# Local attention with 63 keys to a block, one transfer of v a head, and v pooled on TensorE for six pairs

## The chip, the cores and the metric

The kernel runs on one core of one Trainium2 chip. The metric is the device time of one execution in microseconds (us), given as the median of several runs. TensorE (PE) multiplies matrices, VectorE (DVE), ScalarE (ACT) and GpSimd (POOL) work on elements, and SyncE (SP) issues most of the DMA transfers from its own queue, in order. Each engine takes its instructions strictly in the order in which the program lists them.

## The reference

An attention layer feeds two MLP layers. Only the attention and its hand-over are touched by the change, apart from the last output tile.

```python
B, H, S, D = 4, 8, 576, 64;  factor = 4;  Sd = 144
q_d, k_d, v_d = (x.reshape(B, H, Sd, 4, D).mean(axis=3) for x in (q, k, v))
out_up = np.repeat(sm_attn(q_d, k_d, v_d), 4, axis=2)          # pooled attention, 144 x 144
mask = np.abs(pos[:, None] - pos[None, :]) < 4                  # each query sees 7 keys
out_local = softmax(where(mask, scale * q @ k.T, -1e9)) @ v     # local attention
x = (out_up + out_local) as (2304, 512)
x = silu(x @ w_in) @ w_out          # first MLP, 512 -> 2048 -> 512
return elu(x @ w_in2) @ w_out2      # second MLP
```

## The kernel before

**Attention.** The 32 heads are taken as 16 pairs (4 batches of 4 pairs), `attend(i, due)` for pair i. Rows of q and k come in, are transposed on TensorE (L653), and give two attentions. The local one cuts the 576 positions into ten windows of 64 keys, 57 apart. For each of the ten windows and two heads there is one score matmul (L773) into PSUM, a mask is added (in batch 0 by a matmul, L765), softmax runs on DVE, ACT and POOL, the result is transposed (L900) and multiplied with the window of v (L1005). Since ten windows of 64 that are 57 apart don't end at 576, the last starts at 512, and `load_windows` needs two transfers a head, one of nine windows (L614) and one of the last (L618). The pooled attention sums q and k by fours on DVE (L695), has its scores (L847), softmax, transposes (L921) and product (L939). Its v is pooled in one of two ways: for the four pairs of batch 0 (`by_pe`) by 22 matmuls (L708) from the windows already there, with a 0/1 matrix that `pool_matrix` has made as the stationary side and 64 columns of v moving; for the other twelve pairs v is loaded a second time (L608) and summed on POOL (L727, L728) or DVE (L732).

**First MLP.** Its 16 weight blocks of 512 KB (8 of w_in, 8 of w_out) are loaded into a ring of three buffers `ws` and one lent tile (L395, L400), taken apart on ACT (L426, L430) and DVE (L434, L437, L441), and split into a high and a low part (ACT L1101, POOL L1105). A unit (n, f) is 256 tokens by 256 hidden columns: the first product (L1124, 12 matmuls), silu on ACT and DVE (L1152, L1153), a split (L1155, L1158), and the second product (L1172, 12 matmuls). Units of the first tokens start when batch 0 of the attention is done and are then interleaved with the attention of the batches behind it. Six of nine token groups are done so; the rest, and the whole second MLP, follow in a second stage (L1500, L1588, L1590) that is one long run of matmuls.

**What sets the order.** Up to the second stage a list scheduler inside the program orders everything while it is built: each piece is a `Job` with an engine, a planned duration, predecessors and buffers (`Slots`) to take, and the next emitted is the one that can start first by the plan. `D_ROWS`, `D_LOCAL`, `D_V`, `D_W` are planned DMA times, `clock_of` the planned start of each engine, `STICK` a bonus for staying in one tile mode of TensorE, `MOST_H` the number of PSUM banks that first products may hold, `LENT` the weight tiles that attention and weight loads may borrow. Where the plan sees TensorE idle, `fill` puts matmuls on zeros there (L370, 128x512 bf16; nine more, `WARM`, at the start). On the chip nothing is reordered: a piece that is late holds up all that stands behind it on its engine or queue.

## Time and profile before

| | |
|---|---|
| median of 3 runs | 880.45 us (879.81 to 880.62) |
| the profiled execution | 879.63 us, its span in the profile 877.9 us |
| PE busy | 865.9 us, 99% of the span |
| DVE, ACT, POOL busy | 668.7, 543.7, 251.5 us |
| mean granted TensorE clock | 0.996 of full speed |

The time outside the span is 1.7 us. PE counts as busy while it runs fillers and while its clock is low, so 99% does not mean that it does useful work all the time. Times in the trace are counted from the start of the span.

### The profile page before, as it was taken

What the parts mean: (1) busy time and instruction counts of PE and PEld (TensorE: products, weight loads), DVE (VectorE), ACT (ScalarE), POOL (GpSimd) and SP (SyncE); (2) the same over time, 40 slices, a digit from 0 to 9 for tenths busy, and PEclk for the clock granted to TensorE, in tenths of its full rate; (3) what the DMA queues carried; (4) which work ended last, traced back from release to release, by engine and by line L of the source; (5) the groups of instructions that cost most, each with busy time, mean ns of one, the idle gap of its engine ahead of it and who ended that gap; (6) DMA issues with size and microseconds to landing.
All of it is one profiled execution on the core that took longest, in us unless ns stands there. A gap on an engine that the chain in (4) does not pass through costs nothing.

```text
span 877.9 us, 17291 instructions
## 1 busy us (share of the span) xinstructions
PE 865.9 (99%) x6632; PEld 809.7 (92%) x6640; DVE 668.7 (76%) x1255; ACT 543.7 (62%) x1228; POOL 251.5 (29%) x269
## 2 busy tenths in 40 slices
PE   8989999999999999999999999999999999999998
PEld 5779989999999999999999998898998998998986
DVE  8888777776968988979569879389489797493552
ACT  5787675564568568466377387385586684561750
POOL 4488786664103011301024213010141041010000
PEclk9989999999999999999999999999999999999999
DMA  9996377612123436253521340541420531310301
GB/s 170 205 219 173 81 202 180 169 49 97 56 90 121 132 103 221 77 173 125 178 92 52 109 156 1 166 123 60 132 72 37 174 126 37 111 70 37 108 0 72
DMA packets 105522, 100.08 MB, mean 114 GB/s; under 512 B 62240, under 2 KB 92448, under 8 KB 105312
## 3 DMA queue, kind: packets, MB, share of 16 engines
q1 hardware_dynamic: 103072, 98.39, 38.1%
q8 instruction: 52, 0.85, 0.4%
q10 hardware_dynamic: 2368, 0.59, 0.4%
q14 instruction: 30, 0.25, 0.1%
HBM read 75.37 MB, written 23.59 MB: 113 GB/s over the span
## 4 chain that ended last, share of the span: by engine, by line
PE 94%; DVE 2%; DMA 2%; issue 1%; ACT 0%; SPq 0%; POOL 0%; ACTq 0%; POOLq 0%; DVEq 0%
PE b L1500 33%; PE b L1590 22%; PE b L1588 15%; PE b L1172 8%; PE b L1124 7%; PE b L653 1%; PE b L1005 1%; PE b L921 1%; PE b L939 1%; PE b L900 1%; PE b L773 1%; PE b L847 1%; PE b L708 1%; DMA rows<-in_k_dram 1%; DMA ws<-in_moe_w_out_dram 1%; DMA rows<-in_q_dram 1%
## 5 line engine op out<-in xcount | busy, mean ns | idle before, releaser
L1590 PE MATMUL b<-w,grw 128*128 128x512 f32 x384 | 121.2, 389 | 0.0
L1590 PE MATMUL b<-w,ghk 128*128 128x512 f32 x288 | 99.1, 389 | 0.0
L1500 PE MATMUL b<-xhr,xaw 128*128 128x384 f32 x360 | 96.4, 335 | 0.0
L1588 PE MATMUL b<-grw,w 128*128 128x384 f32 x352 | 91.2, 334 | 0.0
L1590 PEld LDWEIGHTS b<-w,grw 128*128 128x128 f32 x384 | 72.1, 188 | 14.9
L1500 PE MATMUL b<-xhr,w 128*128 128x384 f32 x320 | 83.8, 335 | 0.0
L1124 PE MATMUL b<-xh,w 128*128 128x256 f32 x384 | 82.5, 293 | 1.2 <-DVE t L1153 0.7
L1172 PE MATMUL b<-gh,w 128*128 128x256 f32 x384 | 79.6, 288 | 0.0
L1590 PE MATMUL b<-w,glk 128*128 128x512 f32 x192 | 74.8, 389 | 0.0
L1588 PE MATMUL b<-ghk,w 128*128 128x384 f32 x248 | 71.6, 334 | 0.0
L1124 PEld LDWEIGHTS b<-xh,w 128*128 128x128 f32 x384 | 64.7, 194 | 3.0 <-DVE t L1153 0.9
L1500 PE MATMUL b<-xlr,xaw 128*128 128x384 f32 x200 | 66.9, 334 | 0.0
L1500 PEld LDWEIGHTS b<-xhr,xaw 128*128 128x128 f32 x360 | 65.5, 188 | 0.0
L1590 PEld LDWEIGHTS b<-w,ghk 128*128 128x128 f32 x288 | 54.1, 188 | 11.1
L1172 PEld LDWEIGHTS b<-gh,w 128*128 128x128 f32 x384 | 63.3, 191 | 0.7 <-ACT t L1152 0.2
L1588 PEld LDWEIGHTS b<-grw,w 128*128 128x128 f32 x352 | 63.7, 188 | 0.0
L1512 ACT COPY hg<-b 128x384 f32<-128x384 f32 x60 | 28.7, 480 | 52.5 <-PE b L1500 51.9
L1553 DVE SCALAR_TENSOR_TENSOR part<-b,part 128x384 f32<-128x384 f32 (+1 forms) x42 | 25.0, 609 | 44.8 <-PE b L1590 28.4
L1283 DVE TENSOR_TENSOR xlr<-tail,xhr 128x768 fp32r<-128x768 f32 x51 | 49.6, 973 | 11.5 <-ACT xhr L1280 11.2
L1500 PEld LDWEIGHTS b<-xhr,w 128*128 128x128 f32 x320 | 58.0, 188 | 0.2
L1588 PE MATMUL b<-glk,w 128*128 128x384 f32 x168 | 56.1, 334 | 0.0
L1280 ACT CAST xhr<-tail 128x768 fp32r<-128x768 f32 x60 | 50.0, 834 | 7.0 <-DVE tail L1361 4.3
(259 smaller groups left out, 2380.8 us busy)
## 6 DMA issues: line engine op xcount, KB each, us to landing
ws<-in_moe_w_in_dram SPq DMA_DIRECT2D x32, 512.0 KB
ws<-in_moe_w_out_dram SPq DMA_DIRECT2D x31, 512.0 KB
tail<-x SPq DMA_DIRECT2D x24, 384.0 KB
x<-part SPq DMA_DIRECT2D x6, 768.0 KB
out_dram<-part SPq DMA_DIRECT2D x18, 256.0 KB
vw<-in_v_dram SPq DMA_DIRECT2D x28, 144.0 KB
tail<-xd SPq DMA_DIRECT2D x10, 384.0 KB
natv<-in_v_dram SPq DMA_DIRECT2D x22, 144.0 KB
```

The source lines that it names most:

```text
L653: nc.tensor.transpose(bank.tile[:, n * TB:(n + 1) * TB], row(which, c)[:TB], ident[:TB, :TB])
L708: nc.tensor.matmul(bankv[j].tile[:HS, c * D:(c + 1) * D], pooler()[rows_, n, :], vw[rows_, w, :], start=n == 0, stop=n == len(POOLED_BY) - ...
L773: nc.tensor.matmul(held[j].tile[o:o + WIN, c:c + WIN], qT[j * D:(j + 1) * D, q0[w]:q0[w] + WIN], kT[j * D:(j + 1) * D, w0[w]:w0[w] + WIN], ...
L1124: nc.tensor.matmul(ph.tile[:, :NB0], w[a][:, c, :], x_slot(n, c, b_), start=start and m == 0, stop=stop and m == len(products) - 1,)
L1172: nc.tensor.matmul(y[d // 2].tile[:, o:o + NB0], w[m // 2][:, sl], gg(m % 2), start=f == 0 and m == 0 and d % 2 == 0, stop=fin and m == 2, ...
L1280: a = Job("A", ACT_[width], lambda: nc.scalar.copy(hi(), src), preds, gate)
L1283: other=("V", VEC_[width], lambda: nc.vector.tensor_tensor(lo(), src, hi().bitcast(F32), ALU.subtract)),
L1500: nc.tensor.matmul(acc_, a[:, cs], b[:, c, :], start=fresh and c == 0 and m == 0, stop=c == 1 and m == 2, skip_group_check=True,)
L1512: snap[after, j] = [Job("A", ACT_[NB], lambda dst=dst, acc_=acc_: nc.scalar.copy(dst, acc_), [], gate, due=soon)]
L1553: nc.vector.scalar_tensor_tensor(dst, src, sc, dst, op0=ALU.mult, op1=ALU.add)
L1588: nc.tensor.matmul(y[d][:, :NB], wm[:, sl], gm, start=first, stop=last_)
L1590: nc.tensor.matmul(y[d], gm[:, sl], wm, start=first, stop=last_)
```

## The change

Windows have 63 keys, and ten of them 57 apart end at 576, so one transfer brings all ten of a head. The score matmuls keep 64 columns except in the last window, where the 64th column lies behind the end of k: from batch 1 on two more matmuls of one column fill it with some finite score, which the mask takes out. v is pooled on TensorE for the first six pairs. The windows of v are now the stationary side, and 14 or 15 columns of a 0/1 matrix move; the result lies the other way round, so a copy, two transposes and a second copy follow (`turn_v`). Weight tiles are no longer lent to rows of q and k. First products may hold three PSUM banks. The last output tile is computed, evicted and stored in two halves, the second store from ACT's queue. Several planned durations and due times have other values.

```diff
-    PACKED, PE_POOLED, HALVED, CHUNKED, STICK, T_SECOND = 0, 1, 0, 4, 3, 40.0
+    PACKED, PE_POOLED, HALVED, CHUNKED, STICK, T_SECOND = 0, 6, 0, 4, 2, 40.0
...
-    D_ROWS, D_LOCAL, D_V, D_W, S_ROWS, S_LOCAL, X_AFTER = 1.6, 1.9, 1.5, 2.2, 1.1, 2.2, 1
+    D_ROWS, D_LOCAL, D_V, D_W, S_ROWS, S_LOCAL, X_AFTER = 1.6, 2.5, 1.9, 2.7, 1.1, 1.3, 1
...
-    SLACK, MOST_H, N_PSUM, SPLIT_F = 0.05, 2, 16, 3
-    T_MM, T_FIRST, T_PAIR = 0.1185, 38.0, 6.4
+    SLACK, MOST_H, N_PSUM, SPLIT_F = 0.05, 3, 16, 3
+    T_MM, T_FIRST, T_PAIR = 0.1185, 36.0, 6.4
...
-    w0 = [57 * i for i in range(NW - 1)] + [S - WIN]
+    KEYS = WIN - 1
+    w0 = [(KEYS - 6) * i for i in range(NW)]
...
-    LENT = {'rows': [(5, 1), (6, 0), (6, 1)], 'ws': [(7, 0)], 'v': [(7, 1)]}
+    LENT = {'ws': [(7, 0)], 'v': [(7, 1)]}
...
-    clock_of = {"A": 0.0, "V": 4.0, "G": 4.0, "S": 0.0, "P": 5.0, "dma": 0.0, "port": 4.0}
+    clock_of = {"A": 0.0, "V": 4.0, "G": 4.0, "S": 0.0, "P": 3.0, "dma": 0.0, "port": 4.0}
...
-        nc.vector.tensor_copy(m[WIN:P], m[:WIN])
...
-        by_pe = b < PE_POOLED
+        by_pe = i < PE_POOLED
...
-                    vw[j * WIN:(j + 1) * WIN, :NW - 1, :],
-                    bass.AP(tensor=rows.tensor, offset=rows.offset, ap=[[D, WIN], [w0[1] * D, NW - 1], [1, D]]),
+                    vw[j * WIN:j * WIN + KEYS],
+                    bass.AP(tensor=rows.tensor, offset=rows.offset, ap=[[D, KEYS], [w0[1] * D, NW], [1, D]]),
                 )
-                nc.sync.dma_start(vw[j * WIN:(j + 1) * WIN, NW - 1, :], rows[w0[-1]:w0[-1] + WIN, :])
...
-                for n, (w, c) in enumerate(POOLED_BY):
+                for w in range(NW):
+                    m0, m1 = pg[w], pg[w + 1]
                     for j in range(2):
-                        rows_ = slice(j * WIN, j * WIN + pool_rows(w))
                         nc.tensor.matmul(
-                            bankv[j].tile[:HS, c * D:(c + 1) * D], pooler()[rows_, n, :], vw[rows_, w, :],
-                            start=n == 0, stop=n == len(POOLED_BY) - 1, skip_group_check=True,
+                            bankv.tile[j * D:(j + 1) * D, m0:m1], vw[j * WIN:j * WIN + KEYS, w, :],
+                            pooler[j * WIN:j * WIN + KEYS, j, FAC * m0 - w0[w], :m1 - m0], start=True, stop=True, skip_group_check=True,
                         )
...
+            def turn_v():
+                for c in range(2):
+                    nc.tensor.transpose(bankt.tile[:HS, c * P:(c + 1) * P], hvt.tile[:, c * HS:(c + 1) * HS], ident)
...
+                        for c0, k0, n in [(0, w0[w], min(WIN, S - w0[w]))] + [(KEYS, S - 1, 1)] * (w == NW - 1 and b >= MASK_PE):
+                            nc.tensor.matmul(
+                                held[j].tile[o:o + WIN, c + c0:c + c0 + n],
...
+                        if final and k == FP - 1 and d == ny - 1:
+
+                            for c0, queue in ((0, nc.sync), (DM // 2, nc.scalar)):
+                                cs = slice(c0, c0 + DM // 2)
+                                for n_, (wm, gm) in enumerate(((wh, gh), (wh, gl), (wl, gh))):
+                                    nc.tensor.matmul(
+                                        y[d][:, cs], gm[:, d * P:(d + 1) * P], wm[:, cs], start=False, stop=n_ == 2, skip_group_check=True
+                                    )
...
-            prepare(i, dues[pos] - 2.5 if which == 0 else dues[pos + LAG] - 2.5)
+            prepare(i, dues[pos] - 4.0 if which == 0 else dues[pos + LAG] - 4.0)
```

The lines of the changed program have other numbers: L701 is the narrow pooling, L715 its transposes, and L773, L900, L1005, L1124, L1172 are now L776, L903, L1008, L1127, L1175; the fillers are L373.

**TensorE's order at the pooling of the first pair, before.** `rows` are q and k, `ident` makes a transpose, `t` is the zero tile of a filler (two stand here), `natv` holds the 0/1 matrix, `vw` the windows of v. L708 goes on for 22 matmuls.

```order
L921 MATMUL b_97<-ident,ring_120 72x72 x4
L653 MATMUL b_96<-ident,rows 128x96 x5
L653 MATMUL b_93<-ident,rows 128x96 x2
L370 LDWEIGHTS t
L370 MATMUL b_92<-t 128x512
L708 MATMUL b_97<-vw_116,natv 72x64
L708 MATMUL b_99<-vw_116,natv 72x64
```

The same place in the changed program. Five fillers stand where the two rows of L373 are.

```order
L645 MATMUL b_96<-ident,rows 128x96 x5
L645 MATMUL b_93<-ident,rows 128x96 x2
L373 LDWEIGHTS t
L373 MATMUL b_92<-t 128x512
L701 MATMUL b_97<-natv,vw_116 64x15 x2
L701 MATMUL b_97<-natv,vw_116 64x14 x6
L1008 MATMUL b_99<-ring_121,vw_116 64x60 x2
L1008 MATMUL b_94<-ring_121,vw_116 64x57 x2
```

Twenty matmuls with 14 or 15 columns take the place of 22 with 64, and the local product of the first pair (L1008) follows at once, where before it came after two fillers and three transposes. In all there are 60 fillers for 48, and 19 of them for 10 stand ahead of the first transposes of q.

**SP's queue from the last windows of batch 0 on, before.** `yo` and `vw` are windows of v, `ws` and `lent` weight blocks, `lent<-in_q` rows of the first pair of batch 1 in a borrowed weight tile.

```order
L614 DMA yo<-in_v_dram 64x9x64
L618 DMA yo<-in_v_dram 64x64
L400 DMA ws<-in_moe_w_out_dram 128x1024
L395 DMA ws<-in_moe_w_in_dram 128x4x256
L400 DMA lent<-in_moe_w_out_dram 128x1024
L604 DMA lent<-in_q_dram 96x6x64 x2
L604 DMA lent<-in_k_dram 96x6x64 x2
L608 DMA lent<-in_v_dram 72x512 x2
L395 DMA ws<-in_moe_w_in_dram 128x4x256
```

The same stretch in the changed program:

```order
L607 DMA yo<-in_v_dram 63x10x64 x4
L403 DMA ws<-in_moe_w_out_dram 128x1024
L398 DMA ws<-in_moe_w_in_dram 128x4x256
L403 DMA lent<-in_moe_w_out_dram 128x1024
L398 DMA ws<-in_moe_w_in_dram 128x4x256
L597 DMA nat_113<-in_q_dram 96x6x64 x2
L597 DMA nat_114<-in_k_dram 96x6x64 x2
L607 DMA vw_116<-in_v_dram 63x10x64 x2
L403 DMA ws<-in_moe_w_out_dram 128x1024
L597 DMA spare<-in_q_dram 96x6x64 x2
L398 DMA ws<-in_moe_w_in_dram 128x4x256
```

The windows of batch 0 are 8 transfers for 16. The fifth weight block (the second `L398 ws` shown) stands ahead of the rows of batch 1 instead of behind three of their transfers, and the sixth (the second `L403 ws` shown) is row 18 of the queue instead of row 41. The rows of q for pair 5 go into `spare`, which the local product of pair 3 still reads, and the seventh block stands right behind them.

## Rows read from the trace of the kernel before


**Rows 1.** Page of the profile, part 1, TensorE's line

```profile
PE 865.9 (99%) x6632; PEld 809.7 (92%) x6640; DVE 668.7 (76%) x1255; ACT 543.7 (62%) x1228; POOL 251.5 (29%) x269
```

**Rows 2.** Stretches of 4 us: PE, PEld, DVE, ACT, POOL busy, clock, DMA share

```profile
48.00:52.00 4.00, 2.76 (x25) 2.06 (x22) 2.17 (x5) 2.41 (x5) 2.93 (x6) 1.00 1.21 227
52.00:56.00 4.00, 3.11 (x48) 2.73 (x49) 3.74 (x7) 3.83 (x13) 3.90 (x4) 0.55 1.01 217
56.00:60.00 4.00, 4.00 (x25) 3.95 (x24) 3.77 (x11) 3.46 (x11) 3.46 (x5) 0.59 0.59 168
```

**Rows 3.** TensorE's waits in the first 262 us: total, times, longest

```profile
PE b L370 <- issue: 2.0, 3, 1.6
PE b L653 <- DMA nat<-in_q_dram: 1.9, 2, 1.6
...
PE b L921 <- POOL ring L886: 0.9, 2, 0.5
PE b L1124 <- DVE t L1153: 0.7, 1, 0.7
PE b L1124 <- DVE wf L441: 0.5, 1, 0.5
PE b L653 <- DMA rows<-in_q_dram: 0.5, 2, 0.2
```

**Rows 4.** Chain that ended last, first 103 us: start, duration, what

```profile
28.74 1.57 PE b L708 x44
...
30.96 0.69 PE b L900 x5
...
38.83 0.22 PE b L370
...
44.81 5.70 DMA ws<-in_moe_w_out_dram
50.53 0.67 ACT ws L430
...
57.33 0.69 DVE wf L441
...
61.00 0.98 PE b L1124 x6
...
63.57 1.43 PE b L1172 x12
...
98.67 1.44 PE b L1124 x12
100.10 0.74 PE b L773 x40
100.84 1.62 PE b L1172 x12
```

**Rows 5.** TensorE in order of time: first fillers, last L1005 of batch 0

```profile
1.39 3.92 PE L370 MATMUL b<-t 128*128 128x512 bf16 x10 [1.39 <-DVE t L1614]
...
43.91 0.81 PE L1005 MATMUL b<-spare,yo 64*64 64x60 f32 x40
```

**Rows 6.** SP's queue in order of time

```profile
11.68 0.73 SPq L614 DMA_DIRECT2D vw<-in_v_dram  x1
...
24.12 0.64 SPq L618 DMA_DIRECT2D yo<-in_v_dram  x1
...
48.81 1.79 SPq L395 DMA_DIRECT2D ws<-in_moe_w_in_dram  x1
```

**Rows 7.** DVE in order of time: pooled q and k of the first pair of batch 1

```profile
43.69 1.40 DVE L695 TENSOR_REDUCE qkD<-qk 128x144 f32<-128x576 f32 x2
```

**Rows 8.** DMA queues from 186 to 198 us: packets, MB, share of 16 engines

```profile
q1 hardware_dynamic: 1344, 0.33, 12.1%
```

**Rows 9.** The last instructions in order of time

```profile
872.98 2.05 DVE L1553 SCALAR_TENSOR_TENSOR part<-b,part 128x512 f32<-128x512 f32 x3 [9.78 <-PE b L1590]
...
873.70 1.69 SPq L1560 DMA_DIRECT2D out_dram<-part  x3
```

More of the change, by code (lines that the diff above doesn't have):

```diff
@@ L1546, in one, with evict_part @@
                 part_free[h] = []
+                def evict_part(d, c0, c1, queue, h=h, y=y):
+                    dst = part[h][:, d * DM + c0:d * DM + c1]
+                    nc.vector.scalar_tensor_tensor(dst, y[d][:, c0:c1], sc, dst, op0=ALU.mult, op1=ALU.add)
+                    t0 = (2 * duo + h) * NB + d * P
+                    queue.dma_start(out[t0:t0 + P, c0:c1], dst)
                 def evict(d, y=y, h=h, kept=kept):
@@ L1589, in one @@
                             else:
-                                nc.tensor.matmul(y[d], gm[:, sl], wm, start=first, stop=last_)
+                                nc.tensor.matmul(y[d], gm[:, sl], wm, start=first, stop=last_, skip_group_check=final and d == ny - 1)
                         now[0] += T_G / ny
@@ L1671, in attention_moe_moe2_kernel @@
         constants()
+        hpool.take()
         pool_matrix()
-        hpool.take()
         run(g1_jobs[0, 0])
```

84 lines of the change are left out of this document (46 added, 38 removed).

## The prediction

> **What bounds the kernel now.** I read the page first. TensorE is busy for 865.9 of 877.9 us [rows 1], so a saving can only come from work that TensorE no longer has, or from the 12 us and whatever is hidden in "busy". Then the stretches of time. Behind 62 us TensorE waits for 0.9 us in all, twice for a softmax on POOL [rows 3], so whatever lies on another engine there costs next to nothing. Before that it is not so: between 48 and 60 us its idle time is 1.24 and 0.89 us, and from 52 to 60 us the granted clock is 0.55 to 0.59, close to the lower of the two levels (1.2 and 2.4 GHz), after TensorE had been idle in the slice ahead [rows 2]. The list of waits names what was late: a transpose that waits for rows of q (1.9 us in two), and first products that wait for a decoded weight or a PSUM bank [rows 3]. The chain of waits says the same: it goes through a weight block whose transfer was issued at 44.81 us and took 5.70, then through ACT and DVE that decode it, to L1124 at 61.00 us and the first second product, L1172, at 63.57 us [rows 4]. From there on TensorE runs through.
>
> So the end is set by two things: when TensorE gets to that first L1172, and how much it has to do before and after. I make the sum in these terms, over the whole program: TensorE's work, its fillers, its waits, its slow clock, and the tail.
>
> **The work of TensorE.** Wide pooling of v goes: 44 records (22 matmuls) in 1.57 us [rows 4], four times, -6.28 us.
>
> Narrow pooling comes six times: 20 matmuls, so 40 records. No row shows 15 moving columns. The nearest is L773: 40 records with the same 64x64 stationary blocks and 64 columns in 0.74 us [rows 4], 18.5 ns each. If the columns alone counted it would be 15/64 of that, 0.17 us; if it were no cheaper than the wide pooling, 1.57 us. I take 0.74, the row with the same blocks to load: six times, +4.44 us (ends +1.0 and +9.4).
>
> Here a rule speaks against the change. The Trainium skill (TensorEngine Tiling (Array Packing), Instruction Overhead) gives each matmul about 60 cycles however few its columns, so fewer moving columns would buy nothing below 60. By it, at 25 ns for each of 40 records, a pooling would take an estimated 1.0 us and the six together 1.6 us more than in my sum, which would then end at 880.0. L773's 18.5 ns lie below that, since its four array quarters overlap; with 15 columns no run here shows it.
>
> Two transposes of 128 columns a pair: L900 does five in 0.69 us [rows 4], so 0.28, six times +1.66 us.
>
> The last column: two matmuls, four records, for each of twelve pairs; at 18.5 ns +0.89 us (ends 0 and, at the wide pooling's 36 ns, 1.7).
>
> Fillers: twelve more by the order. One in the warm clock takes 0.22 us [rows 4]: +2.64 us. Nine of them stand ahead of the first transposes and push all that TensorE does at the start back by up to 2 us; the first ten run at 0.39 us each [rows 5] as before.
>
> Changes from small array blocks to full ones: an L1172 behind L773 takes 1.62 us, a plain unit of twelve 1.44 [rows 4]. By the order there are 26 of these behind the first second product, for 23: +0.54 us.
>
> Together +4.0 us.
>
> **Waits.** The weight block of the long chain is the sixth. In the new queue it is row 18 instead of 41, and the seventh, issued at 48.81 us before [rows 6], stands two rows behind it. What held them in the queue was issue time, mainly windows and rows of batch 1; now it is their buffers, which the blocks before them leave when DVE has decoded them, by my estimate from DVE's order at about 40 and 44 us. So they come some 5 us sooner, and what waited for them falls away: the 1.9 us (rows of q stand in another place too), 0.5 for the decoded weight, 0.7 for a bank (three may be held now), and 0.5 for the first rows, which the extra fillers cover: -3.6 us. With the idle time goes the slow clock: 3.11 + 4.00 us busy at a mean 0.57 [rows 2] are 4.05 us of work, -3.05 us. What stays is 2.0 us with no visible cause [rows 3].
>
> A new wait: pooled scores of the first pair of batch 1. Their sums on DVE, at 43.69 us before [rows 7], now stand behind five more weight blocks of three operations at up to 0.69 us [rows 4], 9 to 10 us, less about 1.6 us for a copy and a v sum that go. With the later start they come at 54 to 56 us; TensorE gets there at about 55. I take 1.0 us (0 to 2).
>
> Together -5.65 us. If nothing of the old waits fell away this would be +1, if the 2.0 went too, -8.6.
>
> **Costed at nothing.** The windows: 16 transfers for batch 0 keep SP busy from 11.68 to 24.76 us [rows 6], now 8 will. The first weights behind them are not what ACT and DVE wait for at 25 us, since these have the softmax of batch 0; so the 6 us of issue buy nothing by themselves. The v loads and POOL sums of pairs 4 and 5 that go were beside TensorE. The two copies a pair (before two as well) are ACT's and DVE's; their cover is TensorE's next pair, and if it is gone each costs its 0.3 to 0.4 us. Constants: fewer selects on POOL and one DVE copy less, all ahead of the first sums, which now wait for TensorE.
>
> A rule on the windows: by the Trainium skill (DMA: Bandwidth & Descriptors, Why a DMA increments its semaphore by 16 and not by 1) a transfer runs on the largest number of engines up to 16 that divides its outer dimension: 16 for 64 rows, 9 for 63. The trace of before has no transfer of 63 rows. It is one of the rivals.
>
> **The tail.** Three evictions from 872.98 us take 2.05, so the last 0.68, and 2.87 us pass from their end to that of the span [rows 9]. With halves the DVE work grows by about 0.1 us, but the last transfer is 128 KB instead of 256. I take -0.3 us (-0.6 to +0.1).
>
> **Sum.** 4.0 - 5.65 - 0.3 = -2.0 us. The profiled execution took 879.63 us, 1.7 of them outside the span, which nothing here touches, and would take 877.6. The median of the runs is 0.8 us above it, so the median after is 878.4 us.
>
> **Rivals.**
> - *Bought and spent* (chance 0.26): weights come sooner, but DVE, full for most of 52 to 60 us [rows 2], decodes them no sooner. The waits of 3.6 us stay in other places, as idle or as fillers, and only the clock holds: -2.0 + 2.6 to 3.6, so 881 to 882. For it: DVE's busy 3.74 and 3.77 of 4. Against: it was idle for 1.83 us from 48 to 52, waiting for ACT and that weight block.
> - *Head of the queue* (0.14, slower): without lent tiles the q rows of pair 5 go to `spare`, which the last local product of batch 0 reads until 44.7 us [rows 5]. Behind them in SP's queue stand the seventh weight block and all later ones, and behind that block on DVE the first silu. If the last L1008 ends later than 48.8 us, when that block was issued before, weights are no sooner, TensorE idles again and its clock falls: the 3.6 and 3.05 us come back, -2.0 + 6.65, so 885. The fillers at the start push towards it; the shorter poolings (three of them ahead of the last L1008's own inputs, 0.5 us gained each) push back. By my count L1008 ends at 42 to 44 us.
> - *Narrow is not cheaper* (0.05, slower): 1.57 us for each narrow pooling, +5.0, so 883.4.
> - *Windows land late* (0.03, slower): a pair's windows take 12.1% of 16 engines for 12 us, 23 engine-us [rows 8], 1.45 us on all. If fewer engines serve a transfer of 63 rows, the first four pairs each wait, from the point where the delay is over the 1 to 2 us that the windows have in hand. On nine engines it would be 2.6 us, 1.1 more a pair, up to +4.5, so 883. By that page this is the case to expect; no row shows it.
> - *Forecast* (0.52).
>
> **Numbers.** Forecast alone: 874.5 to 878.7. No change that a measurement can tell is within 0.2%, 1.8 us: 878.7 to 882.2. Faster 0.52; same 0.26; slower 0.22. The range takes the lower ends of the waits and of the narrow pooling (878.4 - 3.4 or - 3.0), and on the other side the second rival, the two small slow ones in part, and leaves the fallen clock out: 874.5 to 883.
>
> **What would show it.** Right: a narrow pooling of 0.7 us or less; first L1175 between 59 and 62 us; granted clock 1.0 from 6 us on; sixth block issued at about 40 us; no waits over 0.5 us on TensorE between 44 and 60 but the one on pooled scores. Wrong: first L1175 after 63 us, a slow slice anywhere behind 6 us, the narrow pooling over 1 us, or new waits behind 62 us of more than 1 us in all, where a later order by the plan's new times has its risk.

## The result, and the profile after

The changed kernel took 889.72 us (median of five runs, 889.41 to 894.05) beside 880.45 us before (878.70 to 885.99): a ratio of 1.0116 over the runs, 95% interval 1.0088 to 1.0145 (the two medians alone give 1.0105). It is slower by some 1.1%, where 878.4 us was forecast, and lies outside the range. The runs of one kernel here spread by 1 to 9 us, and the slower of them mostly show the lower mean granted clock of TensorE; this is one of the subjects below. The profiled execution of the changed kernel has a span of 887.7 us, that of before 877.9.

The page's line of TensorE, of the changed kernel (it answers to [rows 1]):

```profile
PE 879.5 (99%) x6779; PEld 820.0 (92%) x6779; DVE 670.9 (76%) x1253; ACT 542.8 (61%) x1234; POOL 239.3 (27%) x258
```

TensorE is busy 13.6 us longer than before, more than the 9.8 us by which the span grew. So it waits less, and the loss is inside "busy": either more work, or the same work at a lower clock.

The stretches of 4 us of the changed kernel (columns as in [rows 2]):

```profile
24.00:28.00 4.00, 4.00 (x104) 3.32 (x104) 3.43 (x9) 3.07 (x9) 1.26 (x1) 1.00 0.89 253
28.00:32.00 4.00, 4.00 (x64) 2.59 (x58) 2.41 (x5) 1.98 (x10) 0.72 (x1) 0.57 0.57 206
...
52.00:56.00 4.00, 2.62 (x18) 1.89 (x18) 4.00 (x8) 4.00 (x11) 4.00 (x5) 0.97 1.00 229
56.00:60.00 4.00, 4.00 (x44) 3.73 (x46) 3.30 (x7) 2.66 (x8) 4.00 (x5) 0.50 0.84 243
60.00:64.00 4.00, 4.00 (x29) 3.37 (x27) 0.95 (x4) 0.94 (x3) 2.69 (x3) 0.50 1.19 226
64.00:68.00 4.00, 4.00 (x57) 3.76 (x57) 2.75 (x7) 3.00 (x11) 0.73 (x1) 0.50 0.49 75
68.00:72.00 4.00, 4.00 (x30) 4.00 (x30) 3.10 (x8) 1.10 (x3) 2.40 (x2) 0.83 0.00 0
```

The granted clock is at its lower level (0.5, 1.2 GHz) twice: for some 3.4 us from 28 us on, with TensorE busy for 4.00 of 4.00 us in the slice ahead, and for some 13.6 us from just before 56 us on, with 1.38 us idle in the slice from 52 to 56 us. One minus the clock, times the length, summed over the slices, is 8.5 us; in [rows 2] it is 3.4 us, in one stretch. This "loss to the clock" is a bound and not a price: a pooling at the lower level took 2.32 us for 1.34 (below), so less than twice as long, and part of a slow stretch can lie where TensorE would otherwise have waited.

It leaves out the start, too. The profile gives the clock as 1.00 from 0 us on, but the first fillers take 0.39 us each ([rows 5]), where later ones take 0.22 [rows 4]. The same 19 fillers, in the same order, took 5.81 us in this execution (the first row of TensorE's order below), and 7.22 us in the profiled execution of the kernel with 64-row transfers, one of the experiments:

```profile
1.38 7.22 PE L373 MATMUL b<-t 128*128 128x512 bf16 x19 [1.38 <-DVE t L1641]
```

So one profiled execution can stand over 1 us later than another from the start on.

TensorE's waits over the whole program (total, times, longest; they answer to [rows 3]):

```profile
PE b L373 <- DVE t L1640: 1.4, 1, 1.4
PE b L1127 <- DVE xa L1025: 1.1, 1, 1.1
PE b L1127 <- DVE ring L812: 0.9, 1, 0.9
PE b L1127 <- POOL xl L1073: 0.3, 1, 0.3
PE b L645 <- DVE ring L812: 0.2, 1, 0.2
```

The waits for rows of q and for a decoded weight are gone, and so are the 2.0 us with no visible cause. Summed over stretches of 20 us up to 860 us, TensorE is idle for 4.2 us; before it was 8.4.

TensorE in order of time, of the changed kernel (start, duration; some rows of several windows):

```profile
1.39 5.81 PE L373 MATMUL b<-t 128*128 128x512 bf16 x19 [1.39 <-DVE t L1640]
7.04 0.58 PE L645 MATMUL b<-ident,nat 96*128 96x96 f32 x5
...
23.29 0.38 PE L715 MATMUL b<-ident,natv 128*72 128x128 f32 x2
23.51 0.38 PE L903 MATMUL b<-ident,ring 128*128 128x128 f32 x2
...
25.10 1.34 PE L701 MATMUL b<-natv,vw 63*64 63x15 f32 x40
...
46.78 1.34 PE L701 MATMUL b<-natv,vw 63*64 63x15 f32 x40
48.05 0.39 PE L1127 MATMUL b<-xh,w 128*128 128x256 f32 x1
...
58.22 2.32 PE L701 MATMUL b<-natv,vw 63*64 63x15 f32 x40
...
68.42 0.41 PE L1175 MATMUL b<-gh,w 128*128 128x256 f32 x1
```

A record is one entry of the profile; the 20 float32 matmuls of a pooling make 40. Forty narrow records (L701) take 1.34 us where the clock is up, and 2.32 at the lower level; 0.74 was forecast. Rows of TensorE overlap, so what a row keeps the engine for is better read from its start to the next start: 1.27 us for a narrow pooling (46.78 to 48.05). The two transposes (L715) have a row of 0.38 us, but the next row starts 0.22 us after theirs (23.29 to 23.51); 0.28 was forecast. The first second product stands at 68.42 us; before it stood at 63.4 (the first start of L1172; the chain of [rows 4] enters its run at 63.57). Two marks divide the span into three parts:

| from, to | before, us | after, us |
|---|---|---|
| start to first second product (L1172, L1175) | 63.4 | 68.4 |
| to the first product behind it, L1500, now L1503 | 184.0 | 188.4 |
| to the end of the span | 630.5 | 630.9 |

So 5.0 us are lost ahead of the first mark, 4.4 between the first and the second, and 0.4 behind.

### The profile page after: what moved, and what is told of

It is laid out like the page before. It is cut to its first block, busy times and chain, and to the rows that moved or that the text cites. A ratio compares the mean times of both kernels' runs of the same rounds, so it can differ in the third digit from the quotient of the medians.

```text
span 887.7 us, 17520 instructions
## 1 busy us (share of the span) xinstructions
PE 879.5 (99%) x6779; PEld 820.0 (92%) x6779; DVE 670.9 (76%) x1253; ACT 542.8 (61%) x1234; POOL 239.3 (27%) x258
## 4 chain that ended last, share of the span: by engine, by line
PE 88%; DVE 0%; DVEq 0%; issue 0%
PE b L1503 33%; PE b L1616 22%; PE b L1614 15%; PE b L1175 6%; PE b L1127 6%; PE b L645 1%; PE b L776 1%; PE b L1008 1%; PE b L924 1%; PE b L850 1%; PE b L942 1%; PE b L903 1%; DVE part L1562 0%; DVE part L1553 0%; DVEq L1776 0%
## 5 line engine op out<-in xcount | busy, mean ns | idle before, releaser
L1503 PE MATMUL b<-xhr,xaw 128*128 128x384 f32 x360 | 96.4, 335 | 0.0
L1127 PE MATMUL b<-xh,w 128*128 128x256 f32 x384 | 84.4, 298 | 1.9 <-DVE xa L1025 1.1
L1503 PE MATMUL b<-xhr,w 128*128 128x384 f32 x320 | 83.8, 335 | 0.0
L1175 PE MATMUL b<-gh,w 128*128 128x256 f32 x384 | 80.2, 290 | 0.0
L1127 PEld LDWEIGHTS b<-xh,w 128*128 128x128 f32 x384 | 65.7, 197 | 4.4 <-DVE xa L1025 1.2
L1503 PE MATMUL b<-xlr,xaw 128*128 128x384 f32 x200 | 66.9, 334 | 0.0
L1503 PEld LDWEIGHTS b<-xhr,xaw 128*128 128x128 f32 x360 | 65.5, 188 | 0.0
L1616 PEld LDWEIGHTS b<-w,ghk 128*128 128x128 f32 x288 | 54.1, 188 | 11.1
L1175 PEld LDWEIGHTS b<-gh,w 128*128 128x128 f32 x384 | 63.7, 192 | 0.6 <-issue 0.6
L1503 PEld LDWEIGHTS b<-xhr,w 128*128 128x128 f32 x320 | 58.0, 188 | 0.2
L1175 PE MATMUL b<-gl,w 128*128 128x256 f32 x192 | 54.4, 283 | 0.0
```

The source lines that it names most:

```text
L1127: nc.tensor.matmul(ph.tile[:, :NB0], w[a][:, c, :], x_slot(n, c, b_), start=start and m == 0, stop=stop and m == len(products) - 1,)
L1175: nc.tensor.matmul(y[d // 2].tile[:, o:o + NB0], w[m // 2][:, sl], gg(m % 2), start=f == 0 and m == 0 and d % 2 == 0, stop=fin and m == 2, ...
L1503: nc.tensor.matmul(acc_, a[:, cs], b[:, c, :], start=fresh and c == 0 and m == 0, stop=c == 1 and m == 2, skip_group_check=True,)
L1616: nc.tensor.matmul(y[d], gm[:, sl], wm, start=first, stop=last_, skip_group_check=final and d == ny - 1)
```

## The experiments

Fifteen further kernels ran, and the changed one a second time. Unless it is said otherwise an edit stands on the changed kernel. Many edits leave the order of the instructions on every engine as it is; others make the planner write a new order, and that matters: the stretch between the two marks then came out up to 17 us longer than before, whatever the edit was for. The table has for each kernel the median, the ratio to before measured beside it, the first two parts of the table above, the idle time and the loss to the clock as defined above (both summed over 20 us stretches of the profiled execution up to 860 us). The last four columns are of one execution each, the median and the ratio of all runs.

| kernel | order | us | ratio [95%] | first | second | idle | clock |
|---|---|---|---|---|---|---|---|
| before | its own | 880.45 | 1 | 63.4 | 184.0 | 8.4 | 3.4 |
| after | its own | 889.72 | 1.0116 [1.0088, 1.0145] | 68.4 | 188.4 | 4.2 | 8.6 |
| after again | as after | 889.05 | 1.0107 [1.0077, 1.0137] | 67.1 | 188.0 | 5.3 | 7.0 |
| 64-row transfers | as after | 885.65 | 1.0051 [1.0025, 1.0077] | 67.1 | 187.9 | 5.0 | 5.2 |
| padded | as after | 884.84 | 1.0050 [1.0027, 1.0073] | 64.3 | 187.9 | 6.0 | 0.0 |
| padded, first four pairs | as after | 884.43 | 1.0059 [1.0037, 1.0081] | 68.9 | 188.6 | 5.4 | 6.8 |
| padded, last two pairs | as after | 887.95 | 1.0077 [1.0042, 1.0112] | 64.4 | 187.9 | 4.2 | 3.6 |
| padded, end of before | as after | 884.43 | 1.0049 [1.0032, 1.0066] | 64.1 | 187.9 | 4.6 | 0.0 |
| padded, pooled twice | as after | 890.04 | 1.0102 [1.0073, 1.0132] | 71.1 | 188.0 | 5.1 | 1.8 |
| padded, no opening fillers | as after | 882.63 | 1.0027 [1.0009, 1.0045] | 61.3 | 187.9 | 5.9 | 0.0 |
| padded, one piece | as after | 883.55 | 1.0045 [1.0030, 1.0059] | 63.8 | 187.1 | 5.9 | 0.0 |
| parts together | as after | 883.35 | 1.0038 [1.0019, 1.0057] | 64.0 | 187.9 | 7.6 | 1.8 |
| six wide | new | 898.13 | 1.0191 [1.0140, 1.0242] | 57.7 | 200.9 | 11.1 | 10.4 |
| old numbers | new | 888.39 | 1.0086 [1.0060, 1.0111] | 62.3 | 192.4 | 8.7 | 0.0 |
| four quadrants | new | 896.19 | 1.0187 [1.0154, 1.0220] | 60.7 | 200.6 | 14.7 | 5.2 |
| four quadrants, 64 rows | new | 897.47 | 1.0199 [1.0165, 1.0232] | 62.0 | 200.4 | 14.3 | 7.0 |
| before, new numbers | new | 890.72 | 1.0128 [1.0089, 1.0167] | 62.0 | 192.5 | 11.7 | 3.6 |
| four pairs, old numbers | new | 885.29 | 1.0058 [1.0026, 1.0091] | 63.6 | 188.7 | 6.2 | 0.0 |

My first theory was that the narrow records let the clock fall. The rivals: that the waits at 52 to 56 us do it whatever the pooling is; that transfers of 63 rows land late; that the planner's new numbers are the loss; later, chance.

**Six wide poolings.** The pooling of before for the same six pairs:

```
-                            bankv.tile[j * D:(j + 1) * D, m0:m1], vw[j * WIN:j * WIN + KEYS, w, :],
-                            pooler[j * WIN:j * WIN + KEYS, j, FAC * m0 - w0[w], :m1 - m0], start=True, ...
+                            bankv[j].tile[:HS, c * D:(c + 1) * D], pooler()[rows_, n, :], vw[rows_, w, :],
+                            start=n == 0, stop=n == len(POOLED_BY) - 1, skip_group_check=True,
```

> The changed kernel with one part taken back: the six pairs are pooled as before, with the values moving (22 records a pair into two banks, two copies, no transposes). The theory 'narrow' says that the granted clock fell to 0.5 at 28 to 32 us and stayed there from 56 to 69 us because records of 14 and 15 columns keep TensorE too lightly loaded, although it hardly waits: then both low stretches shrink to the one of before (about 7 us), and the time falls by 3 to 5 us, to about 885 to 887. The theory 'waits' says that the 1.4 us of waits at 52 to 56 us make the clock fall whatever the pooling is: then the price alone changes, six times 1.57 us against six times 1.27 + 0.28 us, that is +0.1 us, and the time stays within 1.5 us of 889.7.

It took 898.13 us. The price of a wide pooling is again 1.65 us for 44 records, and no low stretch is left in the first 80 us; the first second product comes at 57.7 us, the earliest of all. But the planner wrote another order, and in the second stretch it loses 16.9 us to before, behind it another 7.1: waits for POOL and ACT in the softmax (some 4.6 us) and low stretches between 80 and 140 us are part of it. The time fits neither theory's number, and shows that an edit which makes a new order can't be read by its total.

**64-row transfers.**

```
-                    vw[j * WIN:j * WIN + KEYS],
+                    vw[j * WIN:j * WIN + r],
```

Here `r` is 64, but 63 for the last head of v.

> The changed kernel, but each window transfer brings 64 rows to a window (the last row is not used by anything), still in one transfer a head; only the very last head of v keeps 63. The theory '63 rows' says that a transfer with 63 partitions is spread over fewer DMA engines than one with 64, so that windows and the weights behind them land late: then the last attention of the first batch and the first second product come 2 to 5 us earlier and the time falls to 885 to 888. All other theories expect no difference beyond 0.5 us before the first second product, and 888 to 891 us in all.

SP's queue in the changed kernel, then in this one (start, duration):

```profile
11.84 6.67 SPq L607 DMA_DIRECT2D vw<-in_v_dram  x4
18.56 4.74 SPq L607 DMA_DIRECT2D yo<-in_v_dram  x4
...
41.32 0.35 SPq L403 DMA_DIRECT2D ws<-in_moe_w_out_dram  x1
...
45.13 0.39 SPq L398 DMA_DIRECT2D ws<-in_moe_w_in_dram  x1
```

```profile
11.76 3.85 SPq L608 DMA_DIRECT2D vw<-in_v_dram  x4
15.65 3.88 SPq L608 DMA_DIRECT2D yo<-in_v_dram  x4
...
41.30 0.35 SPq L403 DMA_DIRECT2D ws<-in_moe_w_out_dram  x1
...
45.11 0.39 SPq L398 DMA_DIRECT2D ws<-in_moe_w_in_dram  x1
```

Eight transfers hold SP for 11.4 us with 63 rows and for 7.7 with 64. From 18 to 20 us, stretch by stretch, the changed kernel moves 116 GB/s and this one 190:

```profile
18.00:20.00 2.00, 1.86 (x21) 1.57 (x21) 2.00 (x5) 1.81 (x5) 0.46 (x1) 1.00 0.53 116
```

```profile
18.00:20.00 2.00, 1.78 (x53) 1.32 (x51) 2.00 (x6) 1.64 (x6) 1.86 (x2) 1.00 1.31 190
```

The ratio 0.61 is near 9/16 (0.56). That agrees with the rule of the Trainium skill (DMA: Bandwidth & Descriptors, Why a DMA increments its semaphore by 16 and not by 1), by which 63 rows are served by 9 engines and 64 by 16. But the transfers are not what is waited for: the sixth and seventh weight block go out at 41.30 and 45.11 us in place of 41.32 and 45.13, and the first second product at 67.1 us is where it was in the second profile of the changed kernel. Still the median is 4 us lower, and the low stretch at 28 us was absent in the profile. Its ten runs lie in two groups, 883.5 to 884.5 with a mean granted clock of 0.997 or more, and 886.8 to 888.9 with 0.992 to 0.996. None of the eleven runs of the changed kernel (five above, six below) is in the first group. So the records stay as narrow and the order stays the same, and yet the clock holds in half of the runs. That chance alone did this is unlikely; by which way the transfers could have done it no run shows. With four quadrants 64 rows gained nothing (below).

**Padded.** The same records with up to 64 moving columns; later windows write over the surplus:

```
+                        c0 = j * WIN + (FAC * m0 - w0[w]) * (WIN // FAC)
+                        n = min(WIN, P - c0)
-                            bankv.tile[j * D:(j + 1) * D, m0:m1], vw[j * WIN:j * WIN + KEYS, w, :],
-                            pooler[j * WIN:j * WIN + KEYS, j, FAC * m0 - w0[w], :m1 - m0], start=True, ...
+                            bankv.tile[j * D:(j + 1) * D, m0:m0 + n], vw[j * WIN:j * WIN + KEYS, w, :],
+                            natv[j * WIN:j * WIN + KEYS, c0:c0 + n], start=True, ...
```

> The changed kernel with the same 20 narrow records a pair, but each with up to 64 moving columns in place of 14 or 15 (the further columns land where a later window, or nobody, writes). The order of the instructions is the same. If the price of a narrow record is that of its weights or of its issue, the 40 records of the first and second pair still take about 1.3 us, if it is that of its columns they take 2 us or more. The theory 'narrow' (the clock falls for want of columns) expects the low stretch at 28 to 32 us to go and the long one at 56 to 69 us to shorten, and a time of 885 to 888. The theory 'waits' expects both stretches where they are and 889 to 892 us.

A pooling of the padded kernel, then its stretches:

```profile
26.11 1.38 PE L703 MATMUL b<-natv,vw 63*64 63x64 f32 x40 [0.25 <-ACT spare L932]
```

```profile
28.00:32.00 4.00, 3.10 (x91) 2.60 (x88) 1.72 (x4) 1.49 (x5) 1.17 (x2) 1.00 0.21 82
...
52.00:56.00 4.00, 2.97 (x61) 2.41 (x60) 3.97 (x8) 4.00 (x12) 3.29 (x4) 1.00 0.93 218
56.00:60.00 4.00, 3.57 (x55) 2.93 (x54) 3.29 (x6) 3.02 (x7) 4.00 (x5) 1.00 0.76 208
60.00:64.00 4.00, 4.00 (x73) 3.53 (x72) 3.46 (x9) 3.25 (x15) 3.71 (x5) 1.00 1.04 238
```

Four times the columns cost 0.04 us a pooling, and the clock stays up, although TensorE is idle for 1.03 us at 52 to 56 us, where 1.38 were idle in the changed kernel. The ten runs lie between 883.66 and 886.70; the eleven of the changed kernel lie between 887.20 and 894.05. The mean granted clock is 0.997 or more in each of the 44 runs of the five kernels that have all six poolings padded and 63 rows (this one and four below), and 0.986 to 0.996 in the eleven. So in this order the padding takes the loss away, and 4 to 5 us are the clock's. That is about half of the 8.6 us in the table: TensorE is busy for 6.4 us less (873.1 us), but waits 1.8 us more, and the span is 4.6 us shorter.

**Old numbers.** Transfer costs, clock start, lent tiles, head start and jobs held as before; six narrow pairs, 63 rows and the divided end stay:

```
-    LENT = {'ws': [(7, 0)], 'v': [(7, 1)]}
+    LENT = {'rows': [(5, 1), (6, 0), (6, 1)], 'ws': [(7, 0)], 'v': [(7, 1)]}
...
-    clock_of = {"A": 0.0, "V": 4.0, "G": 4.0, "S": 0.0, "P": 3.0, "dma": 0.0, "port": 4.0}
+    clock_of = {"A": 0.0, "V": 4.0, "G": 4.0, "S": 0.0, "P": 5.0, "dma": 0.0, "port": 4.0}
```

> The changed kernel with the planner's numbers of before (the costs of transfers, the start of its TensorE clock at 5.0 instead of 3.0, the lent row buffers, the head start of the second-layer weights of 2.5 instead of 4.0, two jobs held instead of three), but six narrow pairs, 63 rows and the divided tail kept. The theory 'plan' says that the loss comes from the new numbers, which let the transposes start 1.4 us later and put more fillers in front: then first transposes at 5.7 us, first second product at 62 to 64 us, and 881 to 884 us in all. The theories 'narrow' and '63 rows' expect the low clock to stay, the first second product at 66 us or later, and 886 us or more.

The first transposes are back at 5.72 us, the clock never falls, and yet it takes 888.39 us: 8.7 us idle, and 192.4 us in the second stretch. So with this pooling the old numbers are no better, and the theory "plan" fails for the total.

It also limits the theory "narrow". The six poolings are as narrow as in the changed kernel, and the slice with most of the second and all of the third is as full:

```profile
23.60 1.34 PE L701 MATMUL b<-natv,vw 63*64 63x15 f32 x40
...
24.00:28.00 4.00, 4.00 (x108) 3.58 (x108) 3.11 (x7) 3.03 (x9) 0.00 (x0) 1.00 1.05 349
```

But the mean granted clock is 0.999 or 1.000 in all nine runs. Narrow records alone don't bring the clock down; it takes them in the changed kernel's order.

**After again.**

> The changed kernel once more, unchanged, with more runs and a second profile. The theory 'chance' says that the two low stretches of the clock come and go from run to run, as the runs with 64 rows did (about 884 and about 888 us): then some runs lie at 884 to 886, and the second profile need not show the stretch at 28 to 32 us. The theories 'narrow' and '63 rows' say that they belong to the kernel: all runs at 889 or more, and both stretches again in the profile.

All six runs lie between 887.20 and 892.35 ("all at 889 or more" was too narrow: three lie below), and both stretches are there again:

```profile
28.00:32.00 4.00, 3.78 (x54) 2.42 (x46) 2.23 (x5) 1.97 (x10) 0.72 (x1) 0.57 0.37 143
...
60.00:64.00 4.00, 4.00 (x27) 3.22 (x25) 0.97 (x4) 1.12 (x3) 2.51 (x3) 0.50 1.13 211
```

They belong to the kernel, and the theory "chance" falls in its plain form. How long they last does vary: the late one lasted some 10 us here, and the mean clock of the six runs is 0.986 to 0.996.

**Four quadrants.** Windows of the two halves take turns, the second half goes to the other half of the columns, each head has its own bank:

```
-                for w in range(NW):
+                for w in [c * (NW // 2) + n for n in range(NW // 2) for c in range(2)]:
                     m0, m1 = pg[w], pg[w + 1]
                     for j in range(2):
+                        p_ = (j + w // (NW // 2)) % 2 * D
                         nc.tensor.matmul(
-                            bankv.tile[j * D:(j + 1) * D, m0:m1], ...
+                            bankv[j].tile[p_:p_ + D, m0:m1], ...
```

> The changed kernel with the same narrow records in another order and place: windows of the first and the second half of the sequence take turns, a head's second half goes to the other half of TensorE's columns, and each head has its own bank, so that four records in a row stand in four different quadrants, as those of the scores do (0.74 us for 40 records); two copies a head into the turned tile in place of one. The theory 'quadrants' says that 40 records cost 1.27 us and not 0.74 because only two quadrants are used in turn: then they take 0.7 to 0.85 us, and the time falls by 2 to 3 us at the same clock. The theory 'columns' says that a record of 14 or 15 columns costs what its weights cost: 1.2 to 1.3 us again, and no gain beyond 1 us.

A pooling of this kernel:

```profile
25.09 0.77 PE L702 MATMUL b<-natv,vw 63*64 63x15 f32 x40
```

A quadrant is here which half of the rows a record's operands lie in, with which half of the columns its result goes to: two by two, four. The same forty records take 0.77 us, 19 ns each, in place of 1.28 to 1.34. So the price goes with the quadrants that take turns, not with the columns. The edit also gives the two heads a PSUM bank each; the wide pooling has two banks as well and takes 36 ns a record (1.57 us for 44, [rows 4]), so two banks alone don't make it. Four quadrants in one bank were not run. The first second product comes at 60.7 us, 3.6 us ahead of the padded kernel, but this is no measure of the gain: in the new order only five of the six poolings stand ahead of it. The total, 896.19 us, failed the expectation: the extra bank and copies made a new order, which loses 12.7 us to the padded kernel in the second stretch.

**Four quadrants and 64 rows.** Both edits.

> Both at once: the records in four quadrants and window transfers of 64 rows. If the two gains are apart from each other, the time is that of the run with 64 rows less 2 to 3 us, 881 to 883.5; if the narrow records set the clock, shorter ones may keep it up and the gain is larger. If neither holds, 885 to 886.

897.47 us: none of the three sums came about, and 64 rows gained nothing here.

**Before with the new numbers.** The kernel before, with the changed numbers alone.

> The kernel before with nothing but the planner's new numbers (costs of transfers, the TensorE clock starting at 3.0, the three lent row buffers gone, a head start of 4.0, three jobs held in place of two); pooling, windows and tail as before. The theory 'plan' expects the loss here: first transposes at 7 us in place of 5.7, nine more fillers (2 us) and 884 us or more. The theory that the narrow records and the clock are the loss expects 879 to 882.

890.72 us, as slow as the changed kernel, though no narrow record is in it, and as the theory "plan" expected. Its waits (TensorE, over the program) begin with

```profile
PE b L900 <- POOL ring L784: 3.2, 2, 1.8
PE b L1124 <- POOL w L1105: 1.5, 1, 1.5
```

and the first of them, two waits for POOL in the softmax, stands behind the first second product. That product comes at 62.0 us, earlier than before in spite of the later start; what is lost is lost behind it, 8.5 us of it in the second stretch. So numbers and kernel belong together: the old numbers with the new pooling lose 8 us, the new numbers with the old pooling 11. It doesn't show that the numbers are the loss in the changed kernel: that one's waits are few, and its own loss in the second stretch is 4.4 us.

**Padded, first four pairs, and last two pairs.** `n` is the padded width for `i < 4`, or for `i >= 4`, and `m1 - m0` otherwise.

> The changed kernel with records of up to 64 columns, as in the padded run, but in the first four of the six pairs only (poolings at 21 to 34 us); the order of the instructions is the same. The theory 'narrow' says that each low stretch of the clock comes from the narrow records just ahead of it: then the stretch at 28 to 32 us is gone and the one from 56 us on is there as in the changed kernel, 4 to 5 us of loss, and the time is 886 to 888. The theory 'chance' expects no relation to which pairs are padded. The theory 'early stretch sets the late one' (a first fall shifts what comes behind) expects both to go, and 884 to 885.5.

> The other half: records of up to 64 columns in the last two pairs only (poolings at 46.8 and 58 us), 14 or 15 in the first four. 'Narrow' expects the stretch at 28 to 32 us as in the changed kernel (3 us of loss) and the one from 56 us on gone, 886 to 888. 'Early stretch sets the late one' expects both stretches to stay, 888.5 to 890. Whatever the clock does, the 40 records of a pair take 1.25 to 1.4 us at the full clock.

The stretches of the first, then of the second:

```profile
28.00:32.00 4.00, 2.80 (x74) 2.03 (x68) 1.49 (x4) 1.15 (x4) 0.73 (x1) 1.00 0.26 95
...
56.00:60.00 4.00, 3.69 (x37) 3.31 (x37) 3.33 (x7) 3.03 (x9) 4.00 (x5) 0.58 0.84 226
60.00:64.00 4.00, 4.00 (x37) 3.37 (x36) 1.10 (x4) 1.14 (x3) 3.31 (x4) 0.50 1.06 238
```

```profile
28.00:32.00 4.00, 4.00 (x63) 2.58 (x56) 2.39 (x5) 1.99 (x10) 0.72 (x1) 0.57 0.62 215
...
56.00:60.00 4.00, 4.00 (x51) 3.67 (x52) 3.26 (x6) 2.70 (x8) 4.00 (x5) 0.61 0.91 257
60.00:64.00 4.00, 4.00 (x72) 3.53 (x73) 2.50 (x8) 2.75 (x12) 2.72 (x3) 1.00 1.12 234
```

With the first four padded the stretch at 28 us is gone and the late one is there. With the last two padded the early one is there, and the late one begins but ends before 60 us, while the padded pooling at 58 us is being run; in the changed kernel, where that pooling is narrow, the clock stays down until 69 us. That is "narrow", half by half, in one execution each.

The runs don't bear it out. The profile of the first is of the slowest of its ten runs (890.02 us). Six of the ten lie at 883.3 to 884.5 with a mean clock of 0.997 or more, so there the late stretch is absent or short although the last two poolings are narrow; the median, 884.43, is what "early stretch sets the late one" expected (884 to 885.5) and not "narrow" (886 to 888). The second spreads from 883.1 to 892.3: three of seven runs at a clock of 0.995 or more, and two at 0.989, as low as the changed kernel, although its last two poolings are padded. Its median, 887.95, lies in the range of "narrow" (886 to 888), but seven runs that scatter over 9 us decide nothing. Which of the six poolings brings the clock down stays open; that padding all six keeps it up is shown.

**Padded, with the end of before.** The last tile in one piece: one eviction, one transfer.

> The padded kernel (all six pairs up to 64 columns) with the end of before: the last tile's second product in one piece with one eviction and one transfer, in place of two halves. From the last full-width record of the second product to the end of the span the changed kernel took 5.3 us, before 4.9. If the halves cost this, it is 4.9 to 5.0 again and the time 0.3 to 0.5 us below the padded run's 884.8; if the prediction was right that halves save 0.3, it is 5.5 or more.

DVE in order of time in the changed kernel, then in this one:

```profile
882.39 1.37 DVE L1562 SCALAR_TENSOR_TENSOR part<-b,part 128x512 f32<-128x512 f32 x2 [9.78 <-PE b L1616]
883.78 0.76 DVE L1553 SCALAR_TENSOR_TENSOR part<-b,part 128x256 f32<-128x256 f32 x2
```

```profile
877.61 2.05 DVE L1564 SCALAR_TENSOR_TENSOR part<-b,part 128x512 f32<-128x512 f32 x3 [9.77 <-PE b L1618]
```

From the start of these evictions to the end of the span it is 5.3 us in the changed kernel and 5.2 here (span 882.8), 4.9 before. The halves neither save nor cost what a run can tell.

**Four pairs, old numbers.** Four narrow, padded pairs, old numbers, 64 rows, end of before.

> A try at a version that beats both: four narrow pairs in place of six (as many as before pooled on TensorE), the planner's numbers of before, 64-row window transfers, up to 64 columns a record, and the end of before. By the ledger it has 4 times 1.74 us of pooling and transposes in place of 4 times 1.6 of before, the one-column records, and no low stretch. If what is left of the loss is the work added on TensorE, it ends at 878 to 881. If a plan that was not searched for anew costs some us of waits, as the runs with wide pooling and with the new numbers alone did, it ends at 885 to 892.

885.29 us; the case of the plan that was not searched anew. TensorE waits 1.7 us in one place for nothing visible.

**Padded, pooled twice.** Each of the six poolings done twice in a row.

> The padded kernel with each of the six poolings done twice in a row (40 records more a pair, the same values written again); the order of everything else is the same. If a pooling's 1.3 us lie wholly on the path that sets the end, the time rises by six times 1.3 us, 7 to 8.5 us over the padded run, to 892 to 893 us; then the 0.5 us a pair by which the forecast was short count in full. If waits behind them take part of it (TensorE waits 4 to 5 us in the first 100 us), the rise is 3 to 6 us. If TensorE is not the bound there, less than 2 us.

```profile
27.23 2.54 PE L703 MATMUL b<-natv,vw 63*64 63x64 f32 x80 [0.25 <-ACT spare L936]
```

80 records take 2.54 us, 40 took 1.38, so the addition is 6 times 1.16, 7.0 us. The median rose by 5.2 us; the span of the profiled execution, the slowest of the four, by 6.9, of which up to 1.8 are a low stretch that the padded profile has not. So some 5 of 7 us lie on the path, all ahead of the first mark. Of the rest 0.9 us shows as shorter waits (6.0 to 5.1); in the table below waits are a term of their own.

**Padded, without the opening fillers.** `WARM = 0` in place of 9.

> The padded kernel without the nine fillers that open the program; the order of everything else is the same. In the padded run 19 fillers kept TensorE from 1.39 us on and the first transposes began at 8.05 us, where before they began at 5.67 us, as soon as their rows had landed. If the added fillers are work on the path, the first transposes begin at 5.7 to 6.3 us and the time falls by 1.5 to 2.5 us, to 882.5 to 883.5. If what they delay waits for something else anyway, the time stays within 0.7 us of the padded run.

The first transposes begin at 5.67 us, the first second product at 61.3 in place of 64.3, and the time is 882.63 us: 2.2 us less, as expected of work on the path. (The profile has 3.0 us; the start of the padded execution was a late one, 8.05 us.)

**Padded, one piece.** In batches 1 to 3 the last window's scores in one product over keys shifted by one.

```
-                        for c0, k0, n in [(0, w0[w], min(WIN, S - w0[w]))] + [(KEYS, S - 1, 1)] * (...):
+                        for c0, k0, n in [(0, min(w0[w], S - WIN), WIN if b >= MASK_PE else min(WIN, S - w0[w]))]:
```

> The padded kernel without the separate column: in batches 1 to 3 the last window's scores are one product of 64 columns again, over keys shifted by one (so the scores of that window are not the reference's; everything else is computed). The order of the rest is the same. From the first second product to the first product of the second part the changed kernel and all its variants of the same order took 188.0 us, before 184.0. If the separate columns are what was added there, this stretch is 186.7 to 187.1 (the score records of a pair take 0.74 us again in place of 0.85, eleven times) and the rest must lie in the new waits and in the order; if it is much less than 186.5 they cost more than their records; if 188.0, nothing.

The chain's row for a pair's scores in the changed kernel, then here:

```profile
105.33 0.85 PE b L776 x41
```

```profile
100.26 0.74 PE b L778 x40
```

0.11 us a pair; the second stretch is 187.1 us, for 187.9. So the separate columns cost 0.9 us there, their records and no more.

**Parts together.** Padded, no opening fillers, 64 rows, end of before.

> The padded kernel with everything together that the runs showed to help or not to harm with the order kept: no opening fillers, window transfers of 64 rows, the end of before. By the single runs it takes 882.6 us less 0.4 for the end; the transfers save nothing where the clock is up. So 881.5 to 882.6, still 0.2 to 0.4% slower than before; if it ends below 880, the parts help each other, and if above 883.5, one of them harms here.

883.35 us, where 881.5 to 882.6 was expected: they don't add up. In the profiled execution, at 884.50 us one of the slower, a low stretch of 1.8 us and 7.6 us of idle time came back; but the five fastest runs, at 883.0 to 883.1 with a clock of 0.999 or more, miss the range as well. No version here beats the kernel before.

## Why the prediction was wrong

By its own terms, in us of the profiled executions (the forecast's sum is -2.0; its terms of work make +3.9 where it says +4.0, which changes nothing):

| term | forecast | measured | from |
|---|---|---|---|
| wide pooling goes | -6.3 | -6.3 | [rows 4] |
| narrow pooling | +4.4 | +7.6 | 6 x 1.27, at the upper clock |
| two transposes | +1.7 | +1.3 | 6 x 0.22, at the upper clock |
| last column | +0.9 | +1.3 | 12 x 0.11 |
| twelve fillers | +2.6 | +2.6 | as forecast; nine of them: 2.2 in a run |
| changes of block size | +0.5 | +0.5 | as forecast; not measured |
| waits | -2.6 | -4.2 | 8.4 to 4.2 |
| slow clock | -3.05 | +5.2 | 3.4 to 8.6, a bound |
| tail | -0.3 | +0.4 | 4.9 to 5.3 |

The measured column makes +8.4, beside 9.8 in the spans. For the padded kernel the same column, with waits at -2.4 and the clock at -3.4, makes +1.6 beside 5.2. So 1.4 and 3.6 us stay without a term; the clock's term, a bound, and the start, which it leaves out, are the weak ones. The account names the terms that failed and does not close.

All four signs of being wrong that the prediction names came: the first L1175 behind 63 us, slow slices behind 6 us, a narrow pooling over 1 us, and a new wait of 1.1 us behind 62 us.

**The step that failed first is the clock**: "With the idle time goes the slow clock." The idle time went, by more than forecast, and the clock was low for two and a half times as long. It fell at 28 us with no idle slice ahead of it, in a stretch full of narrow poolings, and stayed low over the one at 58 us. With 64 columns in the same records, in the same order, it stayed up, and the time fell by 4 to 5 us. This is shown for the six pairs together, not for the halves, and for this order, not for narrow records as such: with the old numbers they left the clock up. Why this order lets the clock fall is not shown. The step alone does not make the miss: the padded kernel, without the loss, still takes 884.8 us, 6.4 over the forecast and outside its range.

**The second is the narrow pooling's size**, 1.27 us where 0.74 was put, 3.2 us in six. I took L773, since it has "the same blocks to load". It has, but in four quadrants by turns; the pooling uses two. With four it took 0.77 us, about as L773 does. The rival "Narrow is not cheaper" thus had the mechanism (1.27 us and 0.22 for the transposes, against 1.57), at a chance of 0.05. That its 883.4 us is near the 884.8 of the padded kernel, in which the clock is no longer lost, is in part luck: it put 5.0 us on the poolings. The Trainium skill's 60 cycles a matmul however few its columns (TensorEngine Tiling (Array Packing), Instruction Overhead), by which I estimated 1.0 us, is nearer than the row I took. That few columns save nothing holds here (1.34 us with 15, 1.38 with up to 64); the 25 ns that I took for a record does not: 32 ns in two quadrants, 19 in four.

**Right were** the weight blocks (the sixth at 41.32 us, "about 40"), the waits that fall away, the last column's order of size, and the price of the fillers. But the earlier blocks didn't bring the first second product forward: forecast at 59 to 62 us, it came at 68.4, and at 64.3 in the padded kernel. Too small was what I said of the part behind it: 4.4 us are lost there. Most of it is work. More transposes of rows of q and k stand behind the mark than before (the stretch, its length, busy time and number of these transposes on PE and on PEld, clock, DMA; before, then after):

```profile
63.41:247.41 184.00, 12.99 (x103) 10.32 (x103) 1.00 0.48 128
```

```profile
68.42:256.81 188.39, 14.54 (x115) 11.28 (x115) 1.00 0.45 122
```

Ahead of the mark there are 77 of them for 89. Read from each start to the next start, these twelve take 1.0 us, more transposes of other kinds (L715, L903, L924) 1.0, the scores with their separate columns 1.0, the products of the MLP 1.1, of which some 0.4 are the low clock up to 69.3 us. Waits add only 0.2: the one of 1.1 us on DVE for `xa` takes the place of 0.9 us on POOL. The planner's order decides this stretch (187.1 to 200.9 us in the kernels above).

**The other rivals.** *Head of the queue*: not so, the last L1008 of batch 0 ran at 42.6 us. *Windows land late*: the transfers are slower, nobody waited for them; that they bear on the clock is possible (half of the runs with 64 rows) and not shown. *Bought and spent*: DVE was full at 52 to 56 us (4.00 of 4.00) and TensorE waited 1.1 us for it there, but in all the waits fell.

## What to carry to other kernels

Price a small matmul by a row that uses the same number of array quadrants by turns, not only the same blocks: here up to 64 columns cost 0.04 us more than 15, and four quadrants in place of two saved 0.5 us of 1.3. Count the clock as a term of its own, and don't take idle time for its only cause; here wider records at nearly the same price kept it up. Compare the mean clock of all runs, not of one profile: a single execution can show the opposite of the median. Where a planner writes the order, test with edits that leave the order alone, and read the stretch that the edit touches before the total.

## What was not expected of the hardware

- The granted clock fell to 0.5 with TensorE busy for 4.00 of 4.00 us in the slice ahead, where records of 14 and 15 columns were being run; with up to 64 columns and 0.90 us idle in 28 to 32 us it stayed at 1.00. With the same narrow records in another order it stayed up as well, in nine of nine runs.
- Forty records of 63x64 blocks: 1.34 us with 15 columns, 1.38 with up to 64, 0.77 with 15 columns in four quadrants.
- Four window transfers of 63 rows took SP's queue 6.67 us, with 64 rows 3.85.
